# An attention and gated-MLP kernel on one core: two buffers for combined weights, gelu of v in the u gate's memory, weight chunks spaced by TensorE time, low parts kept in DRAM

## The chip, the cores and the metric

The kernel runs on one core of a Trainium2 chip. The metric is the device time of one execution in microseconds (us): before the change 1030.21 us, median of three runs (1029.97 to 1031.48). Engines are named as in the profile: PE is TensorE, DVE is VectorE, ACT is ScalarE, POOL is GpSimd, SP is the engine that issues the DMAs.

## The reference, cut to what matters

Three blocks follow each other: attention with rotated q and k (4 batches, 8 heads, 576 positions, 64 features), a gated MLP, and a low-rank token mix with a channel MLP.

```python
attn = softmax(rotate(q) @ rotate(k).T / 8) @ v          # x: 4 x 576 x 512
h = gelu(x @ w_in); u, vv = h[..., :512], h[..., 512:]   # w_in 512 x 1024
v_n = (vv - mean) / sqrt(var + 1e-6) * g_ln
x = x + (u * (einsum('ts,bsd->btd', w_sg, v_n) + b_sg)) @ w_out
u = x + (x.T @ U @ V).T                                  # rank 32
out = u + relu(u @ w_ch1) @ w_ch2                        # 512 -> 2048 -> 512
```

Everything is float32, and the weights arrive as 64-bit floats.

## The kernel before

**Numbers in two parts.** A matrix product uses a high part in a 32-bit replicated format (ACT copies it) and a low part, the difference (DVE or POOL subtracts it). Three products of parts make one product.

**Stage 1, attention,** fills the first 296 us and isn't touched.

**Stage 2, the gated MLP,** runs batch by batch, b = 0 to 3. PE's order is written out by hand; the order on ACT, DVE, POOL and SP comes from a scheduler that models time. For each batch `v_step` makes the v half, 128 positions at a time (a `gelu` on ACT into a tile `gt`, the mean and variance on DVE, two small POOL steps for the root, two ACT passes, a POOL subtraction into `VL`; for the last 64 positions of two batches together, the tail, `x_tail` splits x first). `u_step` makes a quarter of the u half and writes its gelu into `ug`, 4 x 576 columns (L658). `s_step` is the product over positions; DVE adds the bias and multiplies by `ug` (L670, L671). `o_step` multiplies by w_out and adds into X (L689). `y_step`, `z_step`, `h_step` are the low-rank mix of the batch before (transposes `t`, sums `z`, products `q`, added into X by L738). PSUM has four tiles in rotation, so a PE step waits until the tile of four steps earlier has been read.

**The weights of stage 3** are made ready beside stage 2 by the generator `first_weights`. The two channel weights are cut into 4 groups of 512 hidden columns; each group has 2 matrices and each of these 2 halves, so there are 16 pairs of chunks. A chunk is loaded by SP into one of two `raw` tiles, and turned from 64-bit floats into 32-bit ones in five steps: one on ACT (L769) and four on DVE (L770 to L773). After the second chunk of a pair, four additions on DVE (L780 to L783) form the seven operands of a Strassen product, and SP writes the tile `cb` (896 KB) to the DRAM tensor `COMBO` (L803). There is one `cb` buffer. `more()` calls in the main loop say after which PE step a chunk is begun; what is left over runs behind the last one.

**Stage 3, the channel MLP,** takes three passes over a third of the positions each; a pass has four periods (one for each group), a period has 14 PE products of about 2.1 us (`r` and `a` in names with the period's number: r7x is of period 7). Its order on all engines comes from times written by hand, counted in PE products. `split` (L879) brings the operands of a group: a load from `COMBO` into a staging tile `YH` or `YL`, an ACT copy into the high part (`w1h`, `w2h`), and a DVE or POOL subtraction into the low part (`w1l`, `w2l`, some in `setA`). Before the first period the 14 operands of group 0 pass through six `tmp` tiles, one operand at a time; the adds of `h_step` for batch 2 stand behind them in DVE's order, and the transposes `t` of batch 3 wait for those adds. At a change of pass (in periods 3 and 7) group 0 is split again, and `u_low` subtracts the low parts of the next third's inputs, on POOL.

Of the kernel before, what the change touches and what calls it, by code (L numbers as in the profile page):

```python
# [65 lines left out]
def tile_kernel(ctx: ExitStack, tc: tile.TileContext, qk, vv, tabs, w_in, g_ln, wsgT, b_sg, w_out, u_r, v_r, w1, w2, out):  # L66
# [497 lines left out]
    def other_weights():  # L564
        for k in range(KT):
            tag = ("YH", "YL")[k % 2]
            raw = py.tile([P, 512, 2], U32, tag=tag, name=tag, bufs=2)
            t = p2.tile([P, 7, 256], F32, tag="cb", name="cb", bufs=1).rearrange("p a b -> p (a b)")[:, :512]
# [7 lines left out]
    def gelu(ps, w, pp):  # L576

        t = p2.tile([P, 2, 512], F32, tag="gt", name="gt", bufs=2)
        t = t[:pp, :ps.shape[1], :w]
        nc.scalar.activation(t, ps, AF.Gelu_apprx_tanh)  # L580
        return t
# [16 lines left out]
    def x_tail(b):  # L598

        TAILS[:] = [x.bitcast(F32R).rearrange("p (a b) -> p a b", b=P) for x in (lambda t: (t[:, 0], t[:, 1]))(raw_tile())]  # L600
# [7 lines left out]
    VP = {}  # L608

    def v_step(b, t):  # L610
# [128 lines left out]


    FG = 512
    NG = DH // FG
# [4 lines left out]
    CHAINS = dict(zip(AT1, "xyxzxzx")), dict(zip(AT2, "XyXzXyX"))  # L747
    STARTS = (1, 2, 5), (1, 2, 3, 5)
    COMBO = [[dram.tile([P, 7, 2, HF], F32, name=f"combo{c}_{g}", bufs=1) for g in range(NG)] for c in range(2)]

    def first_weights():
# [23 lines left out]
        def combine(c, cb):  # L775
            at = places[c]
            e = nc.vector
# [46 lines left out]
    def first_u():  # L824
# [4 lines left out]
        def combo(n, a, b):  # L829
            t = p2.tile([P, 2, 512], F32, tag="gt", name="gt", bufs=2)[:, :, :TB]  # L830
            sub(nc.vector, t, a, b)
            return t
# [7 lines left out]
    def channel(before):  # L840
# [37 lines left out]

        def split(c, g, j0, j1, t, stage, load, lo, e):  # L879

# [33 lines left out]
        def period(i):  # L914
# [67 lines left out]
            if i + 1 < NPASS * NG:  # L982
# [3 lines left out]
                for c, j0, j1, load, t, lo, e in (  # L986
# [4 lines left out]
                ):  # L991
                    split(c, h, j0, j1, o + t, stage, o + load, o + lo, e)
            if g == NG - 1 and p + 1 < NPASS:
# [7 lines left out]
                for t, fn in (  # L1001
                    (1.7, lambda: uh(1, b11)), (2.1, lambda: uh(2, b21)), (2.6, lambda: u_low(pool, 1, b11)),
                    (3.4, lambda: combo(5, b12, b11)), (3.85, lambda: combo(6, b22, U[5])), (4.8, lambda: u_low(pool, 2, b21)),
                    (6.6, lambda: uh(6, U[6])), (7.3, lambda: uh(5, U[5])), (9.9, lambda: uh(3, b22)),
                    (13.5, lambda: u_low(pool, 6, U[6])), (14.4, lambda: u_low(pool, 5, U[5])),
                    (15.4, lambda: sub(dve, U[6], b21, U[6])), (15.85, lambda: sub(dve, U[5], b12, b22)),
                    (16.35, lambda: uh(7, U[5])), (16.37, lambda: u_low(pool, 7, U[5])), (16.8, lambda: uh(4, U[6])),
                    (16.81, lambda: u_low(pool, 3, b22)), (16.82, lambda: u_low(pool, 4, U[6])),
                ):
# [34 lines left out]
    fw = first_weights()  # L1044
    more = lambda n=1: [next(fw, None) for _ in range(n)]
    for b in range(B - 1):
        n = b + 1
        for d in range(KT):
            if d == 1 and n > 1:
                x_split(n)  # L1050
            s_step(b, d)
            with ExitStack() as es:
                if b == 0:
                    es.enter_context(tc.issue_after(LAST_G[0].ins))
                next(ow, None)
            if b:
                more()
        run(v_step, n, 0, 1)
        if b == 0:
            run(v_step, n, 2, 3)  # L1060
# [4 lines left out]
        run(o_step, b, 2, 3)  # L1065
        if b > 0:
            if n % 2 == 0:
                x_tail(n)
            run(v_step, n, 2, 3)
        if n < B - 1:  # L1070
            run(y_step, b, 0, 2)
            v_step(n, 4)
            us = iter(range(KT))
            more()
            if n % 2:
                u_step(n, next(us))
            run(z_step, b, *range(NC - 1))
            y_step(b, 4)
            more()
            u_step(n, next(us))  # L1080
            z_step(b, 4)
            u_step(n, next(us))
            run(h_step, b, 0, 1)
            more(2)
            u_step(n, next(us))
            run(h_step, b, 2, 3)
            more(2)
            run(u_step, n, *us)
            more(2)
        else:  # L1090
            v_step(n, 4)
            more(2)
            for k0 in range(KT):
                u_step(n, k0)
                more()
    more(99)
    a, b = B - 2, B - 1
    for d in range(KT):
        s_step(b, d)
        if d < 2:  # L1100
            y_step(a, 2 * d)
        if d == 1:
            first_u()
    run(z_step, a, *range(NC - 1))
    y_step(a, 4)
# [89 lines left out]
```

## Time and profile before

| | us |
|---|---|
| median of three runs | 1030.21 |
| the profiled execution | 1031.87 |
| its span, first to last instruction | 1030.1 |
| PE busy in the span | 890.2 |
| DVE busy | 770.1 |
| PE's longest wait, for DVE before the transposes of batch 3 | 68.7 |
| its second longest, for ACT before the v tail of batch 2 | 32.2 |

A wait is told as "engine, tile, line <- engine, tile, line", with the sum, the number and the longest one. In a timeline the first number is the start from the span's beginning, the second the duration, and a bracket says how long the engine sat idle before and what ended that. The clock row of the page gives the clock that PE was granted, in tenths of 2.4 GHz: 9 stands for all of it, 5 for 1.2 GHz.

### The profile page before, as it was taken

How to read it: one execution, taken by the hardware profiler on the slowest of the kernel's cores; microseconds unless marked ns; L12 is line 12 of the kernel's file. 1: busy time of each engine (PE TensorE's matmuls, PEld its weight loads, DVE VectorE, ACT ScalarE, POOL GpSimd, SP SyncE). 2: the span in 40 equal slices, each digit the busy share in tenths (PEclk: the TensorE clock that was granted, in tenths of full speed). 3: DMA queues.
4: the chain of work that ended last, by engine and by line, in shares of the span. 5: the costliest groups of instructions: out<-in, count | busy, mean ns of one | idle time of the engine just before them, and what ended most of it. 6: DMA issues, size and time to landing. Idle time of an engine off the chain costs nothing. (4 is left out here: it accounts for less than half of the span.)

```text
span 1030.1 us, 14351 instructions
## 1 busy us (share of the span) xinstructions
PE 890.2 (86%) x5279; PEld 806.8 (78%) x5279; DVE 770.1 (75%) x992; ACT 492.2 (48%) x749; POOL 489.4 (48%) x357
## 2 busy tenths in 40 slices
PE   8999999999999999439998101999988999889998
PEld 4778888788879899329987101899988999889998
DVE  6668788989964657637777554588888888998886
ACT  4565666666756442314342003455555555555552
POOL 6996877777456633203342004044455444554431
PEclk9999999999999999759999655999989999999999
DMA  6787777867433003423342445344325443254421
GB/s 181 201 202 193 203 188 177 206 167 182 131 87 118 1 23 131 145 97 105 118 151 77 153 153 179 92 144 122 113 72 185 138 124 109 80 184 143 123 72 62
DMA packets 85777, 137.31 MB, mean 133 GB/s; under 512 B 31094, under 2 KB 48780, under 8 KB 85708
## 3 DMA queue, kind: packets, MB, share of 16 engines
q1 hardware_dynamic: 85408, 136.33, 45.7%
q8 instruction: 42, 0.69, 0.3%
q14 instruction: 27, 0.22, 0.1%
q10 hardware_dynamic: 300, 0.08, 0.0%
HBM read 99.06 MB, written 19.47 MB: 115 GB/s over the span
## 5 line engine op out<-in xcount | busy, mean ns | idle before, releaser
L213 DVE TENSOR_REDUCE MX<-sm 128x1 f32<-128x576 f32 (+1 forms) x160 | 117.1, 748 | 39.8 <-PE sm L208 33.8
L277 PE MATMUL pv<-pc,VV 128*65 128x288 f32 (+1 forms) x516 | 145.7, 405 | 0.0
L250 PE MATMUL st<-Q,K 65*128 65x288 f32 (+3 forms) x640 | 126.2, 320 | 2.8 <-DMA Q<-mt 1.4
L250 PEld LDWEIGHTS st<-Q,K 65*128 65x128 f32 (+3 forms) x640 | 95.1, 178 | 17.1 <-DMA Q<-mt 1.9
L253 ACT ACTIVATE pc<-st 128x576 f32<-128x576 f32 x129 | 83.3, 646 | 31.1 <-PE st L250 28.5
L277 PEld LDWEIGHTS pv<-pc,VV 128*65 128x65 f32 (+1 forms) x516 | 69.3, 137 | 29.1 <-issue 0.2
L819 POOL TENSOR_TENSOR r7l<-tmp,r7h 128x768 fp32r<-128x768 f32 x12 | 25.5, 2126 | 118.6 <-ACT r7h L816 35.6
L208 PE MATMUL sm<-K,Q 128*128 128x288 f32 (+1 forms) x320 | 71.7, 315 | 2.6 <-DVE K L196 1.2
L708 PE MATMUL t<-ident,X 128*128 128x128 f32 x64 | 9.8, 311 | 68.9 <-DVE X L738 68.7
L708 PEld LDWEIGHTS t<-ident,X 128*128 128x128 f32 x64 | 8.7, 162 | 69.5 <-DVE X L738 69.0
L769 ACT ACTIVATE cb<-raw 128x512 f32<-128x512 f32 x32 | 19.6, 662 | 90.3 <-DMA combo<-cb 87.0
L770 DVE TENSOR_SCALAR cb<-cb 128x512 f32<-128x512 f32 x32 | 17.2, 538 | 59.9 <-ACT cb L769 59.8
L819 POOL TENSOR_TENSOR r1l<-tmp,r1h 128x768 fp32r<-128x768 f32 x12 | 23.0, 1921 | 76.7 <-ACT r1h L816 76.7
L172 POOL TENSOR_TENSOR Q<-raw,Q 128x576 fp32r<-128x576 f32 x30 | 45.1, 1504 | 28.6 <-ACT Q L167 28.5
L208 PEld LDWEIGHTS sm<-K,Q 128*128 128x128 f32 (+1 forms) x320 | 50.1, 178 | 8.8 <-ACT Q L194 1.7
L153 POOL TENSOR_TENSOR raw<-raw,tab 128x576 f32<-128x576 f32 x31 | 50.8, 1638 | 2.7 <-DMA raw<-in_qk 2.7
L540 POOL TENSOR_TENSOR GL<-g,GH 128x576 fp32r<-128x576 f32 x16 | 26.8, 1675 | 45.6 <-ACT GH L672 45.6
L155 POOL TENSOR_TENSOR raw<-raw 128x576 f32<-128x576 f32 x31 | 48.1, 1552 | 0.5
L330 DVE TENSOR_TENSOR X<-stage,rb 64x576 f32<-64x576 f32 x30 | 47.1, 1573 | 1.5 <-DMA rb<-rr 1.0
L589 PE MATMUL u<-XH,setA 128*128 128x288 f32 x256 | 46.2, 296 | 0.0
L154 POOL TENSOR_TENSOR raw<-raw,tab 128x576 f32<-128x576 f32 x31 | 44.8, 1444 | 0.0
L431 POOL TENSOR_TENSOR XL<-X,XH 128x576 fp32r<-128x576 f32 x16 | 26.6, 1688 | 31.0 <-ACT XH L428 31.0
(1109 smaller groups left out, 2707.9 us busy)
## 6 DMA issues: line engine op xcount, KB each, us to landing
YH<-combo SPq DMA_DIRECT2D x44, 512.0 KB
raw<-in_qk SPq DMA_DIRECT2D x31, 576.0 KB
raw<-in_w SPq DMA_DIRECT2D x32, 512.0 KB
combo<-cb SPq DMA_DIRECT2D x16, 896.0 KB
YL<-combo SPq DMA_DIRECT2D x22, 512.0 KB
K<-Q SPq DMA_DIRECT2D x30, 288.0 KB
YL<-combo SPq DMA_DIRECT2D x22, 256.0 KB
VV<-in_vv SPq DMA_DIRECT2D x16, 320.0 KB
```

The source lines that it names most:

```text
L153: lambda: e.tensor_tensor(raw[:, 0], raw[:, 0], tab[:, 0], ALU.mult),
L154: lambda: e.tensor_tensor(raw[:, 1], raw[:, 1], tab[:, 1], ALU.mult),
L155: lambda: e.tensor_tensor(raw[:, 0], raw[:, 0], raw[:, 1], ALU.add),
L172: nc.gpsimd.tensor_tensor(Q2[:, :S], rot, f(Q1), ALU.subtract)
L208: nc.tensor.matmul(ps[:TS[t], n, :HALF], Q1[:, t * P:t * P + TS[t]], K1[:, n * HALF:(n + 1) * HALF], start=True, stop=True)
L213: nc.vector.tensor_reduce(MXs[h % 2][:TS[t], t:t + 1], ps[:TS[t], :, :HALF], AX.XY, ALU.max)
L250: nc.tensor.matmul(ps[:kk, n, :HALF], l[:, c * P:c * P + kk], r[:, ns], start=st, stop=not st)
L253: nc.scalar.activation(h2(pc[:kk]), ps[:kk, :, :HALF], AF.Exp, scale=0.125)
L277: nc.tensor.matmul(o, l, r, start=(c == 0 and j == 0), stop=(c == NC - 1 and j == len(pr) - 1))
L330: nc.vector.tensor_tensor(X[b][rows, pr], STAGE.pop(h - 1 + a)[:D], RB[i][:, a], ALU.mult)
L589: nc.tensor.matmul(o, l, rr, start=(first and j == 0), stop=(last and j == n - 1))
L819: return e.tensor_tensor(out, a, b, ALU.subtract)
```

## The change

- `cb` gets two buffers. Of the four additions of a pair, the second and fourth (the old L781 and L783) go to POOL, and the store to `COMBO` follows POOL's last one.
- The tile `gt` (8 KB a partition) is gone. `v_step` puts its gelu into `ug`, in columns 0 to 1023 and 1024 to 2047 in turn. `first_u` uses `raw` tiles in place of `gt`, and `x_tail` a `YH` tile in place of a `raw` tile; the v tail of batch 2 now stands ahead of the transposes of batch 1 in PE's order, and the rest of PE's order is as it was.
- Chunks are begun by a clock: each PE step adds its time, and at every 5.0 us the next chunk is begun, from batch 0's second half on (before: from batch 0's transposes on).
- The low parts of group 0 (14 operands of 256 KB) are written to a DRAM tensor `LOWS` after the first split, and at the two changes of pass they are loaded from there (9 DMAs each time) and not subtracted again.
- At the changes of pass all `u_low` steps run on DVE, and two ACT copies stand earlier.

```diff
-            t = p2.tile([P, 7, 256], F32, tag="cb", name="cb", bufs=1)...
+            t = p2.tile([P, 7, 256], F32, tag="cb", name="cb", bufs=2)...
...
-        hv = gelu(ps[:pp, :nt], DF, pp)
+        slot[0] = 1024 - slot[0]
+        hv = ug.rearrange("p a b -> p (a b)")[:, slot[0]:slot[0] + 1024].rearrange("p (a b) -> p a b", a=2)[:, :nt]
+        gelu(hv, ps[:pp, :nt])
...
+    EVERY = 5.0
...
-            e.tensor_tensor(s1, a21, op[4], ALU.add)
-            e.tensor_tensor(a21, a21, op[1], ALU.subtract)
-            e.tensor_tensor(s2, s1, op[1], ALU.subtract)
-            return e.tensor_tensor(s4, op[2], s2, ALU.subtract)
+            x = e.tensor_tensor(s1, a21, op[4], ALU.add)
+            o.tensor_tensor(a21, a21, op[1], ALU.subtract)
+            x = e.tensor_tensor(s2, s1, op[1], ALU.subtract)
+            o.tensor_tensor(s4, op[2], s2, ALU.subtract)
...
-                    box[0] = p2.tile([P, 7, HF], F32, tag="cb", name="cb", bufs=1)
+                    box[0] = p2.tile([P, 7, HF], F32, tag="cb", name="cb", bufs=2)
...
+            if e is None:
+                for a, b in parts:
+                    at(lo, lambda a=a, b=b: nc.sync.dma_start(f(wslot(c, 1, a, b - a)), flat(LOWS[c][:, a:b])))
+                return
...
+                    if h == 0:
+                        split(c, h, j0, j1, o + t, stage, o + load, o + 7 * c + j1 + 0.05)
...
+                at(t + 4, lambda c=c, j=j: nc.sync.dma_start(LOWS[c][:, j], f(wslot(c, 1, j))))
...
+    def go(us, fn, b, *which):
+        for x in which:
+            fn(b, x)
+            clock[0] += us
+            while clock[0] > 0:
+                next(fw, None)
+                clock[0] -= EVERY
...
-                (1.7, lambda: uh(1, b11)), (2.1, lambda: uh(2, b21)), (2.6, lambda: u_low(pool, 1, b11)),
+                (1.7, lambda: uh(1, b11)), (2.1, lambda: uh(2, b21)), (2.5, lambda: u_low(dve, 1, b11)),
```

Three places show how the rows move. The first is ACT in batch 0, where the v half's last steps meet the gelu of u (u_0 to u_3 are the four PSUM tiles of `u_step`; L645 to L648 split the tail, L84 begins a w_out chunk). Before, u_0's gelu stands several rows higher, ahead of this piece:

```order
L658 ACTIVATE ug<-u_1_3503 128x576
L645 ACTIVATE VH<-gt 64x512
L647 ACTIVATE VT<-gt 64x512
L648 ACTIVATE VT<-gt 64x512
L84 ACTIVATE cb<-YH 128x512
L658 ACTIVATE ug<-u_2_3529 128x576
```

After the change:

```order
L645 ACTIVATE VH<-ug 64x512
L647 ACTIVATE VT<-ug 64x512
L648 ACTIVATE VT<-ug 64x512
L84 ACTIVATE cb<-YH 128x512
L84 ACTIVATE cb<-YL 128x512
L658 ACTIVATE ug<-u_1_3501 128x576
L658 ACTIVATE ug<-u_0_3475 128x576
```

The gelus of u_0 and u_1 now stand behind the tail's last ACT step and two w_out chunks.

The second is DVE at the end of stage 2, with the last chunk's steps, the low parts of group 0 (from `tmp`), and the adds that the transposes of batch 3 wait for (`X<-q`). Before:

```order
L780 TENSOR_TENSOR cb<-cb 128x256
L781 TENSOR_TENSOR cb<-cb 128x256
L782 TENSOR_TENSOR cb<-cb 128x256
L783 TENSOR_TENSOR cb<-cb 128x256
L819 TENSOR_TENSOR w1l<-tmp,w1h 128x512 x2
L819 TENSOR_TENSOR setA_71<-tmp,setA_70 128x512
L819 TENSOR_TENSOR w2l<-tmp,w2h 128x512 x3
L738 TENSOR_TENSOR X<-q_0_5812,X 128x576
```

After, with the adds of batch 3's `o_step` (`X<-w`):

```order
L689 TENSOR_TENSOR X<-w_0_5614,X 128x576
L689 TENSOR_TENSOR X<-w_1_5633,X 128x576
L822 TENSOR_TENSOR w1l<-tmp,w1h 128x512
L689 TENSOR_TENSOR X<-w_2_5670,X 128x576
L822 TENSOR_TENSOR w1l<-tmp,w1h 128x512
L822 TENSOR_TENSOR setA_71<-tmp,setA_70 128x512
L689 TENSOR_TENSOR X<-w_3_5696,X 128x576
L822 TENSOR_TENSOR w2l<-tmp,w2h 128x512 x3
L738 TENSOR_TENSOR X<-q_0_5817,X 128x576
```

No chunk stands between the adds of `o_step` and those of `h_step` any more, and the low parts are mixed with the former.

The third is DVE at the start of period 3, at a change of pass (`tmp<-r3x` is the sum on which a PE product of the period waits). Before:

```order
L935 TENSOR_TENSOR tmp<-r3y,tmp 128x768
L819 TENSOR_TENSOR w2l<-YH,w2h 128x1024
L819 TENSOR_TENSOR w2l<-YL,w2h 128x512
L819 TENSOR_TENSOR tu<-X 128x768
L819 TENSOR_TENSOR tu<-X,tu 128x768
L819 TENSOR_TENSOR w1l<-YH,w1h 128x1024
L935 TENSOR_TENSOR tmp<-r3x,tmp 128x768
```

After:

```order
L942 TENSOR_TENSOR tmp<-r3y,tmp 128x768
L822 TENSOR_TENSOR w2l<-YH,w2h 128x1024
L822 TENSOR_TENSOR setA_72<-X,setA_72 128x768
L822 TENSOR_TENSOR setA_73<-X,setA_73 128x768
L822 TENSOR_TENSOR w2l<-YL,w2h 128x512
L822 TENSOR_TENSOR tu<-X 128x768
L822 TENSOR_TENSOR tu<-X,tu 128x768
L942 TENSOR_TENSOR tmp<-r3x,tmp 128x768
```

Two subtractions came from POOL, and the one into `w1l` is gone. Period 7 reads the same.

## Rows read from the trace of the kernel before

**Rows 1.** The page: PE's busy tenths and its granted clock in 40 slices.

```profile
PE   8999999999999999439998101999988999889998
PEclk9999999999999999759999655999989999999999
```

**Rows 2.** Waits of PE, whole span: us in total, times, longest.

```profile
PE t L708 <- DVE X L738: 68.7, 1, 68.7
PE v L589 <- ACT raw L605: 32.2, 1, 32.2
PE r7x L874 <- DVE tmp L935: 3.2, 1, 3.2
...
PE r4x L874 <- ACT tmp L816: 2.6, 1, 2.6
```

**Rows 3.** Timeline, all engines: the last pair of chunks, and what follows.

```profile
613.43 1.22 ACT L769 ACTIVATE cb<-raw 128x512 f32<-128x512 f32 x2 [10.79 <-DMA combo<-cb]
...
620.00 0.42 DVE L783 TENSOR_TENSOR cb<-cb 128x256 f32<-128x256 f32 x1
...
625.96 0.63 ACT L816 ACTIVATE w1h<-tmp 128x512 fp32r<-128x512 f32 x1 [11.32 <-DMA tmp<-combo]
...
640.36 2.74 DVE L738 TENSOR_TENSOR X<-q,X 128x576 f32<-128x576 f32 x4
...
641.16 3.67 PE L708 MATMUL t<-ident,X 128*128 128x128 f32 x16 [68.74 <-DVE X L738]
```

**Rows 4.** Timeline of PE: the v tail in batch 0 and in batch 2.

```profile
307.04 2.97 PE L589 MATMUL v<-setA,raw 128*128 128x512 f32 x12
...
455.44 5.83 PE L589 MATMUL v<-setA,raw 128*128 128x512 f32 x12 [32.19 <-ACT raw L605]
```

**Rows 5.** Timeline of batch 0: ACT's steps around the u gate, PE's `s_step`.

```profile
316.76 0.65 ACT L658 ACTIVATE ug<-u 128x576 f32<-128x576 f32 x1
...
322.63 0.69 PE L589 MATMUL m<-WS,VH 128*128 128x288 f32 x4
...
323.97 0.63 ACT L648 ACTIVATE VT<-gt 64x512 fp32r<-64x512 f32 x1
...
324.62 0.67 ACT L84 ACTIVATE cb<-YH 128x512 f32<-128x512 f32 x1
```

**Rows 6.** Timeline of PE: batch 2's last `z_step`, beside batch 3's `o_step`.

```profile
560.33 0.40 PE L726 MATMUL z<-YH,U 128*128 128x512 f32 x1
```

**Rows 7.** Windows: PE, PEld, DVE, ACT, POOL busy us; clock; DMA share; GB/s.

```profile
337.00:641.00 304.00, 192.71 (x1281) 180.42 (x1279) 190.06 (x325) 93.03 (x142) 85.47 (x65) 0.83 0.35 113
```

**Rows 8.** Groups, 337 to 641 us: count, busy us, mean ns, idle before.

```profile
L772 DVE SCALAR_TENSOR_TENSOR cb<-raw,cb 128x512 uint32<-128x512 uint32 x32 | 25.1, 791 | 0.5
...
L781 DVE TENSOR_TENSOR cb<-cb 128x256 f32<-128x256 f32 x16 | 10.5, 656 | 0.4
...
L783 DVE TENSOR_TENSOR cb<-cb 128x256 f32<-128x256 f32 x16 | 7.7, 483 | 0.4
...
L606 POOL TENSOR_TENSOR raw<-X,raw 128x256 fp32r<-128x256 f32 x2 | 1.4, 732 | 17.1 <-ACT raw L605 17.1
```

**Rows 9.** Timelines of POOL and DVE at 381 us: a DVE step beside POOL.

```profile
380.69 7.04 POOL L431 TENSOR_TENSOR XL<-X,XH 128x576 fp32r<-128x576 f32 x4 [15.83 <-ACT XH L428]
...
381.13 1.81 DVE L772 SCALAR_TENSOR_TENSOR cb<-raw,cb 128x512 uint32<-128x512 uint32 x1
```

**Rows 10.** Timeline of period 7, at a change of pass.

```profile
870.21 1.22 DVE L819 TENSOR_TENSOR w2l<-YH,w2h 128x1024 fp32r<-128x1024 f32 x1
...
874.50 2.88 DVE L819 TENSOR_TENSOR w2l<-YH,w2h 128x1024 fp32r<-128x1024 f32 x1
...
884.08 0.95 DVE L935 TENSOR_TENSOR tmp<-r7x,tmp 128x768 f32<-128x768 f32 x1
...
885.08 3.70 PE L874 MATMUL r7x<-XL,setA 128*128 128x384 f32 x12 [3.22 <-DVE tmp L935]
```

**Rows 11.** The chain that ended last: a weight load behind two stores of the output.

```profile
903.06 5.37 DMA YH<-combo
```

More of the change, by code (lines that the diff above doesn't have):

```diff
@@ L567, in other_weights @@
             raw = py.tile([P, 512, 2], U32, tag=tag, name=tag, bufs=2)
-            t = p2.tile([P, 7, 256], F32, tag="cb", name="cb", bufs=1).rearrange("p a b -> p (a b)")[:, :512]
+            t = p2.tile([P, 7, 256], F32, tag="cb", name="cb", bufs=2).rearrange("p a b -> p (a b)")[:, :512]
             nc.sync.dma_start(raw.rearrange("p n w -> p (n w)"), w_out[k * P:(k + 1) * P])
@@ L574, in other_weights, with gelu @@
             yield
-    def gelu(ps, w, pp):
-        t = p2.tile([P, 2, 512], F32, tag="gt", name="gt", bufs=2)
-        t = t[:pp, :ps.shape[1], :w]
+    def gelu(t, ps):
         nc.scalar.activation(t, ps, AF.Gelu_apprx_tanh)
@@ L598, in x_tail @@
     def x_tail(b):
-        TAILS[:] = [x.bitcast(F32R).rearrange("p (a b) -> p a b", b=P) for x in (lambda t: (t[:, 0], t[:, 1]))(raw_tile())]
+        TAILS[:] = [x.rearrange("p (a b) -> p a b", b=P) for x in (lambda t: (t[:, 0], t[:, 1]))(py.tile([P, 2, DM], F32R, tag="YH", name="YH", bufs=2))]
         TH, TL = TAILS
@@ L748, in tile_kernel @@
     STARTS = (1, 2, 5), (1, 2, 3, 5)
+    LOWS = [dram.tile([P, 7, FG], F32, name=f"lows{c}", bufs=1) for c in range(2)]
     COMBO = [[dram.tile([P, 7, 2, HF], F32, name=f"combo{c}_{g}", bufs=1) for g in range(NG)] for c in range(2)]
@@ L829, in combo @@
         def combo(n, a, b):
-            t = p2.tile([P, 2, 512], F32, tag="gt", name="gt", bufs=2)[:, :, :TB]
+            t = raw_tile()[:, :, :TB]
             sub(nc.vector, t, a, b)
@@ L877, in product, with split @@
                             )
-        def split(c, g, j0, j1, t, stage, load, lo, e):
+        def split(c, g, j0, j1, t, stage, load, lo, e=None):
             flat = lambda x: x.rearrange("p a b -> p (a b)")
@@ L991, in period @@
                 ):
-                    split(c, h, j0, j1, o + t, stage, o + load, o + lo, e)
+                    if h == 0:
+                        split(c, h, j0, j1, o + t, stage, o + load, o + 7 * c + j1 + 0.05)
+                    else:
+                        split(c, h, j0, j1, o + t, stage, o + load, o + lo, e)
             if g == NG - 1 and p + 1 < NPASS:
@@ L1044, in tile_kernel @@
     fw = first_weights()
-    more = lambda n=1: [next(fw, None) for _ in range(n)]
+    next(fw)
+    clock = [0.0]
+    def go(us, fn, b, *which):
[5 more added lines that the diff above has]
+                clock[0] -= EVERY
     for b in range(B - 1):
@@ L1050, in tile_kernel @@
                 x_split(n)
+            if b:
+                go(3.7, s_step, b, d)
+                continue
             s_step(b, d)
             with ExitStack() as es:
-                if b == 0:
-                    es.enter_context(tc.issue_after(LAST_G[0].ins))
+                es.enter_context(tc.issue_after(LAST_G[0].ins))
                 next(ow, None)
-            if b:
-                more()
-        run(v_step, n, 0, 1)
+        go(2.7, v_step, n, 0, 1)
         if b == 0:
-            run(v_step, n, 2, 3)
+            go(2.7, v_step, n, 2, 3)
         for e in range(2):
@@ L1064, in tile_kernel @@
             o_step(b, e, KT - 1)
-        run(o_step, b, 2, 3)
+        go(4.8, o_step, b, 2, 3)
+        clock[0] += 3.2
         if b > 0:
@@ L1068, in tile_kernel @@
                 x_tail(n)
-            run(v_step, n, 2, 3)
+            go(2.7, v_step, n, 2, 3, 4)
         if n < B - 1:
             run(y_step, b, 0, 2)
-            v_step(n, 4)
             us = iter(range(KT))
-            more()
             if n % 2:
-                u_step(n, next(us))
+                go(3.2, u_step, n, next(us))
             run(z_step, b, *range(NC - 1))
             y_step(b, 4)
-            more()
-            u_step(n, next(us))
+            go(5.9, u_step, n, next(us))
             z_step(b, 4)
-            u_step(n, next(us))
+            go(3.2, u_step, n, next(us))
             run(h_step, b, 0, 1)
-            more(2)
-            u_step(n, next(us))
+            go(4.2, u_step, n, next(us))
             run(h_step, b, 2, 3)
-            more(2)
-            run(u_step, n, *us)
-            more(2)
-        else:
[L1091 to L1096, printed above, removed]
+            go(3.7, u_step, n, *us)
+        else:
+            go(3.2, u_step, n, *range(KT))
     a, b = B - 2, B - 1
     for d in range(KT):
-        s_step(b, d)
+        go(3.7, s_step, b, d)
         if d < 2:
@@ L1103, in tile_kernel @@
             first_u()
+    for _ in fw:
+        pass
     run(z_step, a, *range(NC - 1))
```

17 lines of the change are left out of this document (9 added, 8 removed).

## The prediction

> **What bounds the kernel now.** I read the page first, then PE's waits, then the timeline around the longest one. In the page's slices PE is at nine tenths or more almost everywhere; it falls to 4 and 3 near 420 us and to 1, 0 and 1 near 600 us, and the granted clock falls with it, from 2.4 to 1.2 GHz [rows 1]. The table of waits has the same two holes: 68.7 us before the transposes of batch 3, 32.2 us before the v tail of batch 2 [rows 2]. Everything else in it is small, the largest being 3.2 us at r7x and one like it a pass earlier at r3x, and 2.6 us at r4x and one like it at r8x. So PE bounds the kernel outside two places, and in those the train of weight chunks does.
>
> The timeline says why. ACT waits 10.79 us for the store of `cb` to land before it may write into the one buffer again, works 1.22 us, and DVE's steps follow: 12.0 us for a pair in which nothing overlaps [rows 3]. The last pair is added up at 620.4; the operands of group 0 then pass ACT from 625.96 on, and the adds of `h_step`, behind their low parts, begin at 640.36. The transposes start at 641.16 [rows 3]. The 32.2 us are the same train met from another side: the tail's split wanted a `raw` tile, which is handed out in turn with the chunks' tiles.
>
> My sum follows the start of those transposes, now 641.16, and then the 389 us from there to the end of the span.
>
> **The v tail of batch 2.** It takes a `YH` tile after the change, and those are free by then; the 32.2 us go [rows 2]. After the hole its twelve matmuls took 5.83 us, the same twelve of batch 0 2.97 [rows 4], at the lower and the higher clock [rows 1]. That is 2.9 us more. Sum: -35.1.
>
> **The wait before the transposes.** With 12.0 us a pair and all of it in a row, 16 pairs take 192 us. They now begin with batch 1's v half, and a second buffer takes the store out of the cycle. By the order, DVE has no chunk left between the adds of `o_step` and `h_step`. So the 68.7 us go [rows 2], and two things take their place.
>
> First, staging group 0. It lasted 14.4 us from ACT's first copy to the adds [rows 3]. In the new order ACT's first copy follows the copy of batch 2's last `z_step`, which PE does at 560.33 [rows 6]; without its wait PE would have stood at the transposes at 572.42 (641.16 - 68.74), 12.1 us later. So 14.4 us meet 12.1 us of cover and some 0.7 us until the adds have begun: I take +3. Bounds are 0 (six of 14 operands can be loaded ahead) and 14.4 (staging begins only at the end of `o_step`). Storing the low parts adds 14 DMAs to SP's queue between the loads, each behind a subtraction that the next load of that `tmp` tile waits for anyway, so they cost nothing unless the queue is late; that lies within the same bounds.
>
> Second, DVE has less air. Between 337 us, where the v half of batch 1 begins, and 641 it is busy 190.1 us of 304 [rows 7]. Two of the four additions leave it, 10.5 + 7.7 us [rows 8]; 171.9 stay. POOL gets 32 of them; the nearest row is a subtraction of the same size at 0.73 us [rows 8], so 23.4 us more on 85.5 [rows 7]. While POOL ran 7.04 us in a row, a DVE step that has a mean of 0.79 us took 1.81 [rows 8, 9], so POOL's work can reach DVE. If it does so in full, DVE needs 195.3 us. PE's way from 337 to the transposes is then about 204 us (below), so DVE is filled to 84 to 96%, where it was filled to 63%.
>
> The Trainium skill speaks against this part of the change. "SBUF — State Buffer", section "SBUF: two separate sides", says that VectorE and GpSimd share a port pair as an exclusive lock: a DVE step with two SBUF inputs and a POOL step block each other for the whole instruction. The trace agrees (1.81 against 0.79, rows above). By that rule moving an addition from DVE to POOL saves nothing when they meet, which is the upper figure of 195.3; by the lower one, 171.9, the time would be some 3 us under my forecast.
>
> A queue in order that is 90% full alternates with PE instead of hiding behind it. The lag that this leaves at the transposes is between 0 (171.9 us) and 19: 195.3, plus 14.4 of staging in which DVE mostly waits, plus 13 (its 114 us of idle time in the window less the 101 of PE's two long waits), is 223 us from 341, or 564, against the 544 of the other terms. I take +3, since the chunks are spaced over PE's time and the two numbers only meet at the upper end.
>
> **gelu of v in the u gate's memory.** It adds waits: u's gelu now waits for the last reader of v's. In batch 0 this shows on PE. The product over positions needs the PSUM tile of u_0 read; that gelu ran at 316.76, well ahead of PE's first `s_step` product at 322.63 [rows 5]. In the new order it stands behind the tail's last copy (323.97 + 0.63), two w_out steps of 0.67 and the gelu of u_1. The copy itself comes 1.3 us sooner, since two gelus of 0.65 left from ahead of it. That puts u_0's end at 323.3 + 1.3 + 1.3 = 325.9, or 3.3 us after PE is ready; with no gain ahead it is 4.6. I take +4.0, on everything behind. In batches 1 to 3 other PE work lies between the two gelus, and I count them in DVE's lag.
>
> Sum: 641.2 - 35.1 - 68.7 + 4.0 + 3 + 3 = 547.4 for the start of the transposes. Their sixteen took 3.67 us behind the hole [rows 3]; at the higher clock, by the ratio of rows 4, about 1.8 less.
>
> **The changes of pass.** At period 7 PE waits 3.22 us for a sum on DVE, which stands behind five steps [rows 10] (period 3 alike). The order takes the 1.2 us `w1l` step out and puts two `u_low` steps in, of about 0.95 (the sum's own length, same size), so DVE's own work grows by 0.7. But POOL loses its `u_low` steps, which stretched those five: the `w2l` step took 2.88 us there, and 1.22 four us earlier [rows 10]. Unstretched, what lies between the two sums is about 5.7 us (1.22, four of 0.95, and some 0.7 for the half-size `w2l` step), where it was 9.6 (874.50 to 884.08); one POOL step remains there, which can give back about 1.7, as it cost the `w2l` step. The gain is between 1.6 us and all of the 3.2; I take 2.5 twice, -5. The waits at r4x and r8x stay: ACT waits there for a weight load, which stands behind two stores of the output and takes 5.37 us [rows 11], and both are where they were. The 9 new loads of low parts run beside it. I know no row for their price; at worst they lengthen that wait by the time of one small load, 2 us each pass. Bounds for the whole part: -6.4 and +4.
>
> **Total.** The profiled execution took 1031.9; less 641.2 - 547.4 = 93.8, less 1.8, less 5 it is 931.3. The median of the runs lay 1.7 under the profiled one: 929.6, say **930**.
>
> **Rivals.**
> 1. *DVE becomes the bound, with POOL's lock.* For it: 195 us against 204. Against it: nothing in the trace shows POOL stopping DVE for all of its time. Transposes at 564, so 946.
> 2. *The second buffer doesn't overlap* (loads wait for `raw` tiles, stores for POOL), so the change doesn't do what it says and only the earlier start counts. 12.0 us x 16 from 341 on ends at 533; the 20.7 us from the last addition to the transposes follow [rows 3]: 554, so 936.
> 3. *PE bounds it alone.* No lag, staging hidden, both 3.2 us gone and a few of the small waits as well: transposes at 540, 918 to 922.
> 4. *Slower than before.* POOL's half of the additions waits in POOL's queue behind subtractions that wait for ACT and PE; SP's store waits for it, the next chunk's load stands behind the store, DVE waits for that chunk, and PE for the adds behind it. With the 6.8 us saved behind them, the transposes must start at 650 or later for that; with the 20.7 us behind the last pair, 16 pairs must then take (629 - 341)/16 = 18.0 us each, 6.0 more than the 12.0 without any overlap. At 18.2 the price is 3 us, or 1033. Nothing in the rows makes each pair lose that much.
>
> **How the numbers follow.** Forecast 930 (its own range 923 to 937): 0.56. Rival 1: 0.20. Rival 2: 0.08. Rival 3: 0.13. Rival 4: 0.02, and 0.01 for no change, which here means within 0.2%, about what a measurement of this kernel can tell. Faster by more than that: 0.97. The range reaches down to rival 3 and, with all bounds of the changes of pass, to 916; up through rival 1 with no gain there, 946 + 9 = 955.
>
> **What would show it.** PE's table of waits should lose both long entries; the first `s_step` of batch 0 should show a wait of 3 to 5 us for ACT's gelu of u; the transposes should start between 540 and 555 and wait under 10 us. DVE's busy time up to there should lie between 172 and 195. ACT's wait for the store of `cb`, 10.79 us in a cycle, should be near nothing. At r3x and r7x less than 1.6 us of wait should be left, and 2 to 3 at r4x and r8x. I am wrong if the chunk train is still running when `o_step` of batch 3 begins, if DVE's steps are stretched so that its busy time passes 200, or if a wait that isn't in today's table is longer than 10 us.

## The result, and the profile after

The changed kernel takes 956.24 us (median of four runs, 955.63 to 957.76), the kernel before beside it 1030.85 (1029.97 to 1031.57): a ratio of 0.928, 95% interval 0.926 to 0.930. The forecast was 930, with a range of its own from 923 to 937 and, reaching through its rivals 1 and 3, from 916 to 955. The profiled execution took 956.1 us, its span 954.3.

The page, PE and its granted clock, to be held against [rows 1]:

```profile
PE   9999999999999897997988759999999999799998
PEclk9999999999999998997999979999999999999999
```

The two holes are gone. What is left are shallow dips, the deepest in slice 24 (549 to 573 us), ahead of the transposes of batch 3. PE's waits, whole span (engine, tile, line <- whom; us in total, times, longest), against [rows 2]:

```profile
PE t L708 <- DVE X L738: 7.8, 1, 7.8
PE z L726 <- ACT YH L710: 6.4, 1, 6.4
PE t L708 <- DVE X L689: 4.2, 3, 2.5
PE r8x L877 <- ACT tmp L819: 3.2, 1, 3.2
PE w L587 <- POOL GL L540: 2.9, 2, 1.6
PE m L587 <- ACT ug L658: 2.8, 1, 2.8
PE m L587 <- DVE g L670: 2.5, 1, 2.5
PE r4x L877 <- ACT tmp L819: 2.1, 1, 2.1
```

The transposes of batch 3 start at 572.29; the forecast had 547.4. From there to the end of the span it is 382.0 us (388.9 before), as forecast. So the miss of 25 us lies ahead of the transposes; what is left of the 26.2 between the medians is that the forecast put the median 1.7 us under the profiled execution, and here the two agree within 0.2. From the starts of PE's stages in the two timelines:

| PE's stretch, from its start to that of the next | before | after | change | forecast |
|---|---|---|---|---|
| batch 0: u and m (the u gate) | 27.7 | 32.0 | +4.3 | +4.0 |
| batch 0: w | 15.7 | 13.9 | -1.8 | 0 |
| batch 0: transposes to the next m | 18.5 | 25.9 | +7.4 | part of +3 (lag) |
| batch 1: second v half, tail, transposes, z | 47.6 | 21.7 | -25.9 | -35.1 |
| batch 2: w and v | 18.3 | 21.4 | +3.2 | 0 |
| batches 2 and 3: z and w | 17.9 | 20.9 | +3.0 | 0 |
| q to the transposes of batch 3 | 72.3 | 10.8 | -61.5 | -68.7 + 3 |
| all other stretches, with stage 1 | | | +2.4 | 0 |

The window from 337 us to the transposes (columns as in [rows 7]):

```profile
337.00:572.29 235.29, 202.52 (x1319) 189.80 (x1318) 204.94 (x294) 92.98 (x141) 110.41 (x97) 0.94 0.48 156
```

PE stands idle in 32.8 of the 235.3 us, the waits above and smaller ones; the forecast has 16.5 (the 10.5 of small waits that [rows 7] leaves beside the two long ones, and 6 new). PE's busy time is 7.5 us more than before for the same work (202.5 less 5.1 that lie in the window only because all is later, against 192.7 less the 2.9 that the tail lost at the lower clock), since the granted clock falls behind the waits: 0.94 over the window. The rest, 1.1 us, is a later start. 16.3 + 7.5 + 1.1 is the 24.9.

DVE is busy 204.9 of 235.3 us, 87%, where it was 63%. Its groups and POOL's two additions in this window (count | busy us, mean ns), against [rows 8]:

```profile
L774 DVE SCALAR_TENSOR_TENSOR cb<-raw,cb 128x512 uint32<-128x512 uint32 x32 | 30.9, 967 | 0.9
L775 DVE SCALAR_TENSOR_TENSOR cb<-raw,cb 128x512 uint32<-128x512 uint32 x32 | 28.4, 889 | 0.7
L772 DVE TENSOR_SCALAR cb<-cb 128x512 f32<-128x512 f32 x32 | 22.4, 699 | 6.5 <-ACT cb L771 6.4
L773 DVE TENSOR_SCALAR cb<-cb 128x512 uint32<-128x512 uint32 x32 | 21.8, 685 | 0.7
L671 DVE TENSOR_TENSOR g<-g,ug 128x576 f32<-128x576 f32 x15 | 15.6, 1041 | 0.2
L670 DVE SCALAR_TENSOR_TENSOR g<-m,small,bh 128x576 f32<-128x576 f32 x15 | 12.1, 808 | 0.0
...
L783 POOL TENSOR_TENSOR cb<-cb 128x256 f32<-128x256 f32 x16 | 15.2, 951 | 39.5 <-DVE cb L782 23.6 <-issue 15.5 <-POOL XL L431 0.4
L785 POOL TENSOR_TENSOR cb<-cb 128x256 f32<-128x256 f32 x16 | 14.4, 898 | 3.3 <-DVE cb L784 3.2
```

The four conversion steps took 791, 766, 538 and 473 ns before; that is 21.5 us more over 32 chunks, though the change doesn't touch them. The timeline shows where it comes from (DVE and POOL, the first chunk of the train):

```profile
351.45 0.41 DVE L772 TENSOR_SCALAR cb<-cb 128x512 f32<-128x512 f32 x1
351.60 1.42 POOL L540 TENSOR_TENSOR WOL<-cb,WOH 128x512 fp32r<-128x512 f32 x1 [2.62 <-ACT WOH L572]
351.90 1.40 DVE L773 TENSOR_SCALAR cb<-cb 128x512 uint32<-128x512 uint32 x1
352.98 1.60 POOL L540 TENSOR_TENSOR GL<-g,GH 128x576 fp32r<-128x576 f32 x1
353.34 1.80 DVE L774 SCALAR_TENSOR_TENSOR cb<-raw,cb 128x512 uint32<-128x512 uint32 x1
355.17 0.69 DVE L775 SCALAR_TENSOR_TENSOR cb<-raw,cb 128x512 uint32<-128x512 uint32 x1
```

A step beside POOL takes 1.4 or 1.8 us, the next one of the same size, with POOL at rest, 0.69. The two POOL steps here are no additions; they were in the kernel before.

### The profile page after: what moved, and what is told of

Same layout as the page of the kernel before. It is cut to its first block, busy times and chain, and to the rows that moved or that the text cites. A ratio compares the mean times of both kernels' runs of the same rounds, so it can differ in the third digit from the quotient of the medians.

```text
span 954.3 us, 14383 instructions
## 1 busy us (share of the span) xinstructions
PE 895.8 (94%) x5279; PEld 811.3 (85%) x5279; DVE 773.2 (81%) x964; ACT 492.6 (52%) x749; POOL 468.1 (49%) x365
## 5 line engine op out<-in xcount | busy, mean ns | idle before, releaser
L172 POOL TENSOR_TENSOR Q<-raw,Q 128x576 fp32r<-128x576 f32 x30 | 45.7, 1523 | 30.1 <-ACT Q L167 30.0
L771 ACT ACTIVATE cb<-raw 128x512 f32<-128x512 f32 x32 | 21.5, 674 | 71.3 <-DMA raw<-in_w 61.4
L155 POOL TENSOR_TENSOR raw<-raw 128x576 f32<-128x576 f32 x31 | 47.6, 1537 | 0.5
L587 PE MATMUL u<-XH,setA 128*128 128x288 f32 x256 | 47.6, 303 | 0.0
L819 ACT ACTIVATE w2h<-YL 128x1024 fp32r<-128x1024 f32 (+1 forms) x22 | 18.6, 844 | 48.1 <-DMA YL<-combo 44.6
L587 PE MATMUL m<-WS,VH 128*128 128x288 f32 x192 | 34.6, 304 | 6.6 <-ACT ug L658 2.8
L587 PE MATMUL v<-setA,XH 128*128 128x512 f32 x128 | 39.6, 391 | 1.3 <-DVE X L689 1.3
L587 PEld LDWEIGHTS u<-XH,setA 128*128 128x128 f32 x256 | 39.8, 196 | 0.3
L819 ACT ACTIVATE w2h<-YH 128x1024 fp32r<-128x1024 f32 x22 | 23.2, 1056 | 31.3 <-DMA YH<-combo 20.1
```

Of the source, the lines that this page charges most:

```text
L155: lambda: e.tensor_tensor(raw[:, 0], raw[:, 0], raw[:, 1], ALU.add),
L172: nc.gpsimd.tensor_tensor(Q2[:, :S], rot, f(Q1), ALU.subtract)
L587: nc.tensor.matmul(o, l, rr, start=(first and j == 0), stop=(last and j == n - 1))
```

## The theories

**A.** DVE's queue is full, because POOL's steps stretch DVE's, and PE's small waits and the late end of the chunk train follow. **B.** ACT stands in its queue at raw loads (61.4 us in 23 waits), and the copies that PE needs stand behind them. **C.** The train is spaced by PE's time, and its last store with the staging behind it sets the end. The runs take these apart; times are medians of four runs each. The four lie 0.7 to 5.8 us apart (farthest in e13, e15 and e6), so differences under 2 us are not read, and those under 5 us with care.

## Experiments: POOL and DVE

**e1_adds_dve.**

```diff
-            e, o = nc.vector, nc.gpsimd
+            e, o = nc.vector, nc.vector
```

> The changed kernel with all four additions of a pair on DVE; nothing else is changed. Theory A, DVE's queue is full because POOL's steps stretch DVE's (the four conversion steps take 967, 889, 699 and 685 ns where they took 791, 766, 538 and 473 before, 21.5 us over 32 chunks): without POOL's additions these means go back to within 60 ns of the old ones; DVE gets 32 additions of about 0.45 us, 14 us; its busy time up to the transposes of batch 3 falls from 203.5 to about 196, and the time to 945 to 953. Theory B, ACT's queue in order stands behind raw loads (61.4 us in 23 waits) and what PE needs stands behind it: DVE gives the raw tile back no sooner, so 955 to 960.

Measured: 950.4 us, inside A's numbers, but not for A's reason. The conversion means fell only to 923, 873, 638 and 649 ns, 5 us over 32 chunks, and DVE was busy 205.6 us up to the transposes, not 196. So POOL's new additions are a minor part of the stretch.

**e15_less_only** and **e7_less_dve** move the subtractions as well: e15 has only this edit, e7 this and the one of e1.

```diff
     def less(out, a, b):
-        return nc.gpsimd.tensor_tensor(out, a, b, ALU.subtract)
+        return nc.vector.tensor_tensor(out, a, b, ALU.subtract)
```

> The changed kernel with the four additions of a pair and the subtractions GL, VL, WOL (and WST, once, at the start) on DVE instead of POOL. POOL keeps about 30 us of the 109 up to the transposes of batch 3. If POOL's steps are what stretches DVE's, whichever steps these are, the four conversion steps fall to means of at most 760, 760, 480 and 480 ns (967, 889, 685 and 699 in the changed kernel); if something else stretches them (DMA writes, waits on ACT), they stay over 850 and 640. DVE then does some 34 us more of its own and is stretched by some 33 us less, so its busy time is again near 205 and the time within 6 us of 956, better if POOL's latency (GL and VL: 4.3 us of PE's waits) counted.

> The changed kernel with only GL, VL and WOL on DVE; the two additions of a pair stay on POOL. Moving the additions back alone gave 5.9 us (e1_adds_dve), both together 15.8 (e7_less_dve). If DVE's stretch goes with POOL's busy time, whichever steps fill it, GL, VL and WOL (45 us of POOL) are worth more than the additions (30 us): 9 to 12 us, 944 to 948. If the hand-over of the additions to POOL and back to SP is what counts, 953 to 956.

Measured: e7 940.5 us, e15 943.2, a little better than expected. In e7, the window from 337 us to its transposes at 555.60, and groups in it:

```profile
337.00:555.60 218.60, 196.09 (x1294) 183.95 (x1292) 193.64 (x350) 90.93 (x139) 39.30 (x35) 0.96 0.52 168
```

```profile
L774 DVE SCALAR_TENSOR_TENSOR cb<-raw,cb 128x512 uint32<-128x512 uint32 x32 | 25.6, 803 | 0.5
...
L773 DVE TENSOR_SCALAR cb<-cb 128x512 uint32<-128x512 uint32 x32 | 15.2, 476 | 0.4
L772 DVE TENSOR_SCALAR cb<-cb 128x512 f32<-128x512 f32 x32 | 13.4, 420 | 4.3 <-ACT cb L771 4.2
...
L671 DVE TENSOR_TENSOR g<-g,ug 128x576 f32<-128x576 f32 x14 | 10.5, 750 | 0.1
```

The means fell as far as expected for two of the steps and close to it for the others (803 and 777, where at most 760 was expected). DVE does 35 us more of its own (GL 11.3, VL 8.0, WOL 2.0, the additions 7.2 and 6.7) and is busy 193.6 us, 11 less than in the changed kernel. I had expected the two to cancel; the time is 15.8 us lower, and 13.0 of it is had with the old subtractions alone. Two readings are left: DVE's steps are no longer stretched, or PE no longer waits for POOL's slower results.

**e13_pool_waste** is e7 with useless POOL work:

```diff
+                for _ in range(3):
+                    nc.gpsimd.tensor_tensor(waste, cb[:, at[m]], cb[:, at[m]], ALU.subtract)
```

> e7_less_dve with 96 subtractions on POOL whose results nobody reads (128x256, both inputs in a chunk's converted slot, three per chunk), about 70 us of POOL work, as much as e7 took away. No step on DVE, ACT or PE waits for their results (the buffer of combined weights comes free two pairs later). If e7's 15.8 us are DVE steps that POOL no longer stretches, the conversion means rise again from 803, 777, 476 and 420 ns to 850 or more, 850 or more, 600 or more and 550 or more, and the time from 940.5 to 950 to 962. If the 15.8 us are PE no longer waiting for what POOL is slow to deliver (GL, VL), the time stays at 940 to 945.

Measured: 960.4 us, 19.9 more than e7. The same window, and groups of DVE and POOL, up to its transposes at 575.79:

```profile
337.00:575.79 238.79, 202.88 (x1304) 189.62 (x1302) 219.32 (x350) 91.35 (x140) 114.35 (x131) 0.93 0.47 153
```

```profile
L775 DVE SCALAR_TENSOR_TENSOR cb<-raw,cb 128x512 uint32<-128x512 uint32 x32 | 27.4, 856 | 0.5
...
L773 DVE TENSOR_SCALAR cb<-cb 128x512 f32<-128x512 f32 x32 | 18.6, 580 | 1.8 <-ACT cb L772 1.6
...
L671 DVE TENSOR_TENSOR g<-g,ug 128x576 f32<-128x576 f32 x14 | 12.0, 856 | 0.0
L670 DVE SCALAR_TENSOR_TENSOR g<-m,small,bh 128x576 f32<-128x576 f32 x14 | 11.3, 806 | 0.0
...
L806 POOL TENSOR_TENSOR waste<-cb 128x256 f32<-128x256 f32 x96 | 75.7, 789 | 104.6 <-DVE cb L776 97.1 <-DVE bmv L633 2.5
```

Nobody reads these results, and the whole gain is gone. DVE's busy time rose from 193.6 to 219.3 us: 25.7 us for 75.7 us of POOL, 0.34 us for each. The window is 20.2 us longer, while DVE's idle time in it fell from 25.0 to 19.5 us. Nor did the useless work make POOL's own results late: in this window DVE waits 0.6 us for POOL (2.1 in e7), PE and ACT not at all. One caution: the scheduler orders DVE's queue a little differently here. But the means of the same steps rose as A says, except at L773 of the changed kernel's numbering, where 561 ns stayed below the 600. That POOL's work stretches DVE's, and that this costs the time, is shown.

**e6_shift_out** lightens DVE instead:

```diff
-            nc.vector.tensor_scalar(tu, tu, 5, 2, ALU.logical_shift_left, ALU.logical_shift_right)
```

> The changed kernel without the shifts of the conversion (the third of its five steps, 32 DVE steps, 21.8 us busy), so the combined weights are wrong; loads, stores, ACT's and POOL's steps all stay. Theory A, DVE's full queue is what PE's small waits and the late end of the chunk train come from: DVE busy up to the transposes of batch 3 falls by more than the 21.8, since POOL then meets fewer of its steps; the waits of 1 to 6 us at t, z, w, m and q shrink by half or more, the transposes start at 555 to 562, time 938 to 946. Theory C, the train is spaced by PE's time, and its last store with the staging behind it sets the end whatever DVE does: the train ends within 3 us of where it did, time 951 to 956.

Measured: 947.2 us, between the two. DVE's busy time up to the transposes fell by 17.9 (187.1), less than the 21.8 taken out; the last two conversion steps grew (1031 and 919 ns, 3.0 us more over 32 chunks). The last store came 12 us sooner, so C's "whatever DVE does" is wrong; but 7.4 us of wait before the transposes were left, so DVE's load is not all.

## Experiments: loads, the wait at z, staging

**e3_noload** takes the raw loads away:

```diff
+            if 2 <= j < 28:
+                raws[j] = held[j % 2]
+                return
+            held[j % 2] = raws[j] = bits(raw_tile()...
```

> The changed kernel, but chunks 2 to 27 convert again what the first two loads brought, so their 26 raw loads are left out, and the weights of most groups are wrong. ACT's waits for raw loads (61.4 us in 23 waits) must nearly vanish. Theory B: with them go PE's wait of 6.4 us at z for ACT's copy and most of the 4.2 us at the transposes of batch 0, with the cold matmuls behind them; transposes of batch 3 start at about 556 instead of 572, time about 940. Theory A: DVE's queue is as full as before (busy 200 or more); the time stays within 5 us of 956.

Measured: 951.4 us, 4.8 less. ACT's waits for raw loads went from 61.4 to 4.0 us, the wait at z from 6.4 to 3.4, but the one for `X` at batch 0's transposes rose from 4.2 to 6.3, and DVE stayed as busy (202.6). So the raw loads are worth 5 us, not 16. This is no upper bound for ACT's queue, since waits for the store of `cb` came up, of which the changed kernel has none:

```profile
ACT cb L774 <- DMA combo<-cb: 14.5, 6, 4.8
```

What a raw load does at z shows in ACT's timeline of the changed kernel:

```profile
434.55 1.52 ACT L578 ACTIVATE ug<-v 128x1024 f32<-128x1024 f32 x2
441.59 0.66 ACT L771 ACTIVATE cb<-raw 128x512 f32<-128x512 f32 x1 [5.53 <-DMA raw<-in_w]
442.15 1.92 ACT L710 ACTIVATE YH<-t 128x1024 fp32r<-128x1024 f32 x2
```

The transposes ended at 436.8; ACT could have copied them, but a chunk's first step stood ahead in its queue and waited 5.53 us for the load.

**e4_tail_back** puts the tail back behind the transposes.

```diff
-            go(2.7, v_step, n, 2, 3, 4)
+            go(2.7, v_step, n, 2, 3)
...
             run(y_step, b, 0, 2)
+            if b > 0:
+                go(2.7, v_step, n, 4)
```

> The changed kernel with the v tail of batch 2 behind the transposes of batch 1, where it was in the kernel before; it still takes a YH tile. If PE waits 6.85 us at z because nothing lies between the transposes and the product any more, the tail's 2.8 us are cover again: 3.5 to 4 us of wait are left there, and the time is 2.5 to 4 us lower (952 to 954). If ACT's copy is late because ACT stands at a raw load, and that load moves along with PE, the wait stays at 6 to 7 us and the time at 956.

Measured: 953.2 us. The waits at z fell from 6.85 to 4.9 us only, and those at w of batches 2 and 3 shrank too; the wait at the last transposes grew from 7.8 to 11.4. PE came sooner, staging didn't follow: what PE gains in the middle is partly given back at the end.

**e5_lows_late** moves the stores of the low parts:

```diff
-                at(t + 4, lambda c=c, j=j: nc.sync.dma_start(LOWS...
+                at(1 + 0.1 * (7 * c + j), lambda c=c, j=j: nc.sync.dma_start(LOWS...
```

> The changed kernel with the 14 stores of group 0's low parts put behind h_step, at the start of period 0, instead of between the staging loads. If these stores lengthen staging (16.8 us from ACT's first copy to the adds of h_step; 14.4 in the kernel before, which had none), the wait of 7.8 us before the transposes of batch 3 falls to 5 to 6 and the time to 953 to 954. If staging goes by the loads alone, 956. If the stores then hold up group 1's loads in period 0, slower.

Measured: 953.3 us; the wait fell from 7.8 to 5.9. Staging (ACT's first copy to the adds) lasts 14.2 us here, 16.8 in the changed kernel, 14.4 before [rows 3]. The windows of staging in the changed kernel and then in e5 (the last two columns are the DMA engines' busy share and GB/s):

```profile
560.00:572.00 12.00, 2.96 (x21) 2.48 (x19) 5.00 (x8) 6.58 (x11) 7.14 (x6) 0.75 1.02 375
```

```profile
560.00:568.00 8.00, 3.46 (x25) 2.99 (x23) 5.12 (x6) 5.48 (x9) 7.08 (x6) 0.99 0.82 261
```

With the stores among the loads the DMA engines are full, at 375 GB/s; without them they are not. The edit also takes the stores out of SP's queue, so the share of the two isn't separated, but no wait of SP at a store is listed between the loads.

**e8_every45** and **e9_first2** end the train sooner:

```diff
-    EVERY = 5.0
+    EVERY = 4.5
```

```diff
-    next(fw)
+    for _ in range(3):
+        next(fw)
```

> The changed kernel with EVERY = 4.5 instead of 5.0, so the chunks come denser and the last store of a pair earlier. If the end of the train and staging behind it set the start of the transposes (7.8 us of wait there), that wait falls to under 4 us and the time to 948 to 952. If DVE's fill decides, the waits of PE in batches 1 and 2 grow by as much: 954 to 960.

> The changed kernel with the first two chunks issued before batch 0's products over positions, where DVE is busy 12.4 of 17 us and less before that. All others keep their spacing, so the train is two chunks shorter at its end. If the end of the train sets staging, the last store comes about 8 us sooner, the wait of 7.8 us at the transposes falls to 0 to 3, time 948 to 951. If the two chunks only delay batch 0's gate, and DVE makes up for nothing, 955 to 958.

Measured: 947.5 and 948.5 us. The wait before the transposes is 5.3 and 5.0 us, not below 4 and 3; but the last stores came some 19 and 13 us sooner (528.5 and 534.5 against 547.6), and with them went waits at w ahead of staging. So the end of the train matters, but not by C's chain alone: the transposes came only 8.1 and 6.9 us sooner (564.17 and 565.41 against 572.29). In the changed kernel the chain from the last store (547.6) over SP's loads and ACT's copies to the adds has a DVE step in it:

```profile
548.26 11.49 SPq L889 DMA_DIRECT2D tmp<-combo  x8
```

```profile
554.74 0.63 ACT L819 ACTIVATE w1h<-tmp 128x512 fp32r<-128x512 f32 x1
558.05 1.29 ACT L819 ACTIVATE w1h<-tmp 128x512 fp32r<-128x512 f32 x2 [2.68 <-DMA tmp<-combo]
```

```profile
571.49 2.75 DVE L738 TENSOR_TENSOR X<-q,X 128x576 f32<-128x576 f32 x4
```

ACT's first copy waited for nothing; it stood behind ACT's copy for z. Of the loads only the first went out behind the last store; the second waited until 555.38. SP's waits from 520 to 575 us say for what:

```profile
SPq L806 <- POOL cb L785: 21.7, 3, 18.1
SPq L889 <- DVE XH L822: 6.4, 1, 6.4
```

The last store itself stood 18.1 us in SP's queue until POOL's addition came, and the second load 6.4 us until a step of `first_u` in DVE's queue. So what C names, the end of the train and of staging, hangs on DVE's queue in this trace, which is A's. What held staging in e8 and e9 was not taken apart.

## Experiments: parts undone, and all together

**e12_cb1** (`bufs=2` back to 1 for `cb`) and **e11_pass_undone** (low parts subtracted again at the changes of pass, no `LOWS`, most of `u_low` on POOL as before).

> The changed kernel with one buffer of combined weights instead of two; spacing, POOL's additions and all else stay. If the second buffer does what it says, ACT's waits for the store of cb come back (some 60 us in total, each up to 10, in front of the copies that PE needs), the train ends 10 us or more later and the time is 965 to 980. If loads and DVE's fill held the train anyway, so that the second buffer hides nothing, 955 to 960.

> The changed kernel with the changes of pass as in the kernel before: group 0's low parts are not stored but worked out again, and POOL does most of u's low parts. What the edit is worth lies behind the transposes of batch 3: from there to the end of the span 387 to 389 us instead of 382.0, with waits of about 3.2 at r3x and r7x. Ahead of them staging has no stores between its loads: the wait of 7.8 falls to about 5 as in e5_lows_late. Sum 956.2 + 6 - 3 = 959, between 957 and 961.

Measured: e12 1001.9 us, more than the 965 to 980 expected. ACT's waits for the store are back, 69.3 us, and so is PE's hole:

```profile
ACT cb L771 <- DMA combo<-cb: 69.3, 12, 13.0
```

```profile
PE t L708 <- DVE X L738: 64.6, 1, 64.6
```

The second buffer is thus worth 45.7 us of the 74.6. e11: 957.4 us. The waits at r3x and r7x are 3.2 each again, and from the transposes to the end it is 386.1 us, 4.1 more than with the edit; but staging lasts 15.2 us instead of 16.8, and the transposes start 2.8 sooner. The two nearly cancel.

**e10_all** (the edits of e7, e5 and e9), **e10b_all45** (and `EVERY` = 4.5) and **e14_tail45** (and the edit of e4).

> The changed kernel with three edits together: four additions and the subtractions GL, VL, WOL on DVE (as in e7_less_dve, 940.5), the low parts' stores behind h_step (as in e5_lows_late, -3.0) and the first two chunks before batch 0's products (as in e9_first2, -7.7). If the three act at different places (stretched DVE steps; DMA share in staging; the last store), the sum is 956.2 - 15.8 - 3.0 - 7.7, some of the last already in the first: 930 to 936. If they all shorten the same wait at the transposes, 938 to 941.

> As e10_all, with EVERY = 4.5 as well. With POOL off DVE's back there is air for denser chunks: PE's waits in batches 1 and 2 stay under 10 us in total and the wait at the transposes of batch 3 falls below 2: 926 to 933. If DVE is full again, 1 to 4 us slower than e10_all.

> e10b_all45 (932.2) with the v tail of batch 2 behind the transposes of batch 1, as in e4_tail_back. The wait of 6.7 us at z for ACT's copy is the largest left. If the tail covers it: 3 to 4 us less, 928 to 930. If the wait only moves, or staging takes it back, 931 to 934.

Measured: 936.4, 932.2 and 934.5 us. e10 lies at the upper edge of its first range: the parts share a little of their gain. In e10b 2.4 us of wait are left before the last transposes and 11.3 us at t and z of batches 0 and 1, a little more than expected. e10b beats both kernels: a ratio to the kernel before of 0.905 (0.902 to 0.908), or 24.1 us below the changed kernel. Its longest wait is still at z, 6.0 us for ACT's copy; with the tail behind the transposes (e14) 6.1 us of waits stay there and the time is not lower.

## Why the prediction was wrong, point by point

**Right.** The holes go; the u gate costs 4.3 us (forecast +4.0; but that was all wait, and measured are 2.8 of wait, under the 3 to 5 named, and 1.6 of products at the lower clock behind it, so the number is right in part by luck); ACT's wait for the store of `cb`, 87 us in sum before, is gone, and e12 shows that the second buffer does it. Stage 3 gains the forecast 6.8, but by other parts, so its sum is luck. The transposes were to gain 1.8 and gained nothing (3.67 us before and after, at the lower clock both times). The periods at the two changes of pass gained 6.3 where 5 was forecast (its lower bound of 1.6 each took the POOL step's 1.7 from the wait of 3.2; taken from the 3.9 that its own steps free, it is 2.2). The windows of period 3, before and after:

```profile
739.66:776.16 36.50, 32.90 (x170) 31.99 (x169) 32.42 (x27) 19.09 (x25) 18.52 (x11) 0.91 0.33 104
```

```profile
670.39:702.69 32.30, 30.05 (x170) 29.35 (x169) 27.38 (x28) 18.99 (x25) 4.42 (x2) 1.00 0.65 215
```

The waits at r3x and r7x are down to 0.6 each, 5.2 us together, but 1.7 us each came up at a3X and a7X; what else is gained is PE's busy time, 32.9 to 30.1 us here and 31.1 to 29.9 in period 7, at a granted clock of 1.00 where it was 0.91 and 0.95. e11, with the old waits, has 0.95 in both periods and needs 68.2 us for the two, where the kernel before needed 70.8; so some 2.6 of the 6.3 belong to how the clock fell in the profiled execution of before. The wait at r8x is 3.2, a little over the 2 to 3 named.

**The step that failed: "DVE has less air".** The forecast added the stretch of POOL's *new* work only: "if it does so in full, DVE needs 195.3 us" is 171.9 plus 23.4 of additions. But 171.9 was measured while DVE stood idle for 114 of 304 us. Laid over each other, POOL's and DVE's timelines up to the transposes have 33 of POOL's 86 us in DVE's idle time before, and 18 of 110 after; so POOL's time beside a busy DVE went from 52 to 92 us, and the old subtractions stretch DVE more than they did. Counted over the timelines, for conversion steps that stand alone in a row: 20 of 117 lay beside POOL before, 52 of 122 after, 19 of 124 in e7, 58 of 124 in e13; beside POOL such a step takes 0.49 to 0.74 us more in the changed kernel (0.42 to 1.06, 0.43 to 0.91, 0.69 to 1.43, 0.69 to 1.40). So DVE needed 204.9, the forecast's own line for "wrong" was 200, and rival 1 was nearer, with 946: it had POOL stretching DVE, but by the new work alone. The size of the step, for which the forecast took +3, is e7's 15.8 us; 13.0 of it are had with subtractions that the change never touched. Another sign of being wrong came true with it: the train was still running when batch 3's `o_step` began (542.8), its last addition on DVE began at 545.74. With the 9.2 and 4.8 us of the next two parts, the 12.8 over +3 make 26.8, against 24.9 missed at the transposes, so the three overlap little; in e7 the waits at z (6.1) and before the transposes (9.3) are still there.

The Trainium skill, "SBUF — State Buffer", section "SBUF: two separate sides", was cited as speaking against the additions on POOL; the lock that it describes, between a DVE step with two SBUF inputs and a POOL step that reads SBUF, asks nothing about which steps are new. The traces agree: L671, with two inputs in SBUF, has a mean of 1041 ns in the changed kernel and 856 in e13 where e7 has 750, while L670, which has one of its inputs in PSUM, has 808, 806 and 808.

**The v tail: -35.1 was -25.9.** The forecast asked what the 32.2 us cost, not what they covered. The trace of before answers it: behind the same transposes, which ended at 423.25, ACT and then DVE wrote

```profile
426.73 1.94 ACT L710 ACTIVATE YH<-t 128x1024 fp32r<-128x1024 f32 x2
```

```profile
431.75 1.19 DVE L716 TENSOR_TENSOR YL<-t,YH 128x1024 fp32r<-128x1024 f32 x1
```

so z could not have had its last input before 432.9 even then, 9.7 us after the transposes, and the hole hid it. The change also takes the tail's 3 us out of that place. 6.85 us of waits came up there and some 2.4 of lower clock.

**Staging: +3 was 7.8, and the stores were not free.** It lasts 16.8 us, not 14.4, and its cover is 9.8 us (from ACT's first copy at 554.74 to 564.5, where PE was ready), not 12.1, which was counted from PE's `z_step` (553.25 here) as if the copy followed at once; with the 0.8 us until the adds have begun that makes the 7.8. "They cost nothing unless the queue is late" was said of SP's queue; what was full was the DMA engines. Without the stores staging lasts 14.2 us (e5) or 15.2 (e11), so they are 1.6 to 2.6 of the 16.8.

**Rival 2 was mispriced.** "The second buffer doesn't overlap" was to cost 6 us more than the forecast, 936. e12 takes the overlap away and is 46 us slower: with one buffer the train went on until 596, not 533. That is 15.8 us a pair from 343 on; the 12.0 came from pairs in a row, with little else to do. What lengthened each pair was not taken apart.

**What stays open.** That e1's 5.9 us and e15's 13.0 sum to more than e7's 15.8 was not followed up. How the 15.8 us of e7 divide among the waits at t, z, w and m was not taken apart, and e3's and e4's few us overlap with them. ACT's order, which puts a chunk's first step ahead of the copy that PE needs, was not changed by itself.

## What to carry to other kernels

A step's mean in a profile holds for the load its neighbour had then: before filling an engine's idle time, ask which other engine's work had been using that idle time, and price the old work too, not only the new. When a stall goes, read in the trace what was done during it by others; the last of these is the next wait. Whether a transfer is free is read from the DMA share of its window, not from its queue alone.

## What the runs showed of the hardware

In e13, useless subtractions on POOL cost DVE 0.34 us for each us of POOL (75.7 us of POOL, 25.7 us of DVE), with DVE busy in 92% of the window. POOL stretches DVE steps that read SBUF alone, also those with one tensor input (L772: 420 ns in e7, 699 in the changed kernel). The DVE steps here with an operand in PSUM keep their means in the kernel before, the changed kernel, e7 and e13: L670 806 to 809 ns, L689 748 to 750, L738 749 to 751. POOL's own 128x256 addition took 951 and 898 ns in the changed kernel where the estimate used 732 [rows 8]; DVE does one in 0.42 where nothing holds it up (e7).
